# Twelve empty instructions ahead of VectorE's first fill, and the turn of b1's row five products later

## The chip, the cores and the metric

The kernel runs on one core of a Trainium2 chip. The metric is the device time of one execution in microseconds (us), as the median of the runs shown. Engine names in the profile: PE is TensorE's products and PEld its weight loads, DVE is VectorE, ACT is ScalarE, POOL is GpSimd, and SP is SyncE, which issues most transfers.

## The reference

A block with a local attention that is gated by a feed-forward layer: 2048 tokens, 448 columns, 16 heads of 28, all in bfloat16.

```python
x = A_x                                    # [1, 2048, 448]
xn = _layernorm(x, axis=-1)                # no scale, no shift
# attention: each token sees itself and 7 tokens before it, 2 apart
qkv = xn @ wqkv                            # [2048, 3 * 448]
idx = pos[:, None] - arange(8) * 2         # mask where idx < 0
attn = softmax(q . k[idx] * 28 ** -0.5)    # over the 8
s = (attn . v[idx]) @ wo
# feed-forward, F = 1792
h = gelu(xn @ w1 + b1)
g = silu(h @ w2 + b2)
return x + s * g
```

## The kernel before

The tokens are split into even and odd ones, so that a window with a step of 2 becomes a plain window in each half, and into 16 tiles of 128 tokens. Four tiles make a chunk of 512. Per tile, `norm` (L468) and `stats` (L428) take the row statistics on VectorE, scale x into a bfloat16 tile `xn`, and turn it on TensorE (tiles 0 to 3, against the identity `ident`) or by a transposing transfer (later tiles) into `xnT`, the layout that the products need. Since 448 columns are three blocks of 128 and one of 64, GpSimd copies the last 64 columns of `xn` a second time beside themselves (L480), and the second pair of transposes of each tile waits for that copy. `first_batch` (L605) makes the q, k and v products of tiles 0 and 1 block by block, as soon as half of a tile is turned. Products of the feed-forward layer, scores, weighted values and the output projection follow chunk by chunk; all of them are issued through `product` (L524).

The bias `b1` lies in memory as one row of 1792 numbers. A GpSimd transfer brings it as 14 rows of 128 (`b1r`, in the second buffer of the ring `E`, filled with zeros by GpSimd first: L418 and L419). TensorE turns these rows into a PSUM bank (`f_b1`, L1040 to L1042, task 223) and VectorE copies the 14 columns into `b1` (L1043, task 224). ScalarE reads `b1` first in the first gelu.

The order of the work is written out by hand. Every piece of work is a task of `_Plan`, with an engine, an estimated cost, what it depends on, and what buffers it takes and gives back. `ORDER` (L25) lists the task numbers, and each engine executes its own tasks in that order, so one task's place in the list decides what queues behind it on its engine. Semaphores are placed by the framework from what tasks read and write. `_place` also runs a clock of estimates: a task takes the buffer (a PSUM bank, say) that is estimated to be free earliest, and the warm-up products (tasks 1 to 48, with no use but to keep TensorE busy before x arrives) are left out when their estimated start is over 8.0. A transfer's estimated landing is its issue, its size over a rate, and a `tail`; tails are estimates alone and nothing in the program waits for them.

`zero` (L294) is the last buffer of the ring `h`; VectorE fills it with zeros as its first work (task 126, L1016), and seven rows of it go to memory as padding ahead of v once x's fourth tile has arrived. Behind that fill on VectorE stand the fills of `eps_t` and `half_t`, two of `qk_tok` and one of `v_tok`, and then the statistics of tile 0 (task 86). On TensorE, tasks around the turn are 134 (tile 0's second pair of transposes), 223 (b1's row), 159, 153 and 156 (tile 0's first products), 138 (tile 1's first transposes), 154 and 157 (two more products of tile 0) and 140 (tile 1's second transposes).

Of the kernel before, what the change touches and what calls it, by code (L numbers as in the profile page):

```python
# [11 lines left out]
ACT = mybir.ActivationFunctionType  # L12

HOP = 0.10
TABLE = 1.28
SWITCH = 0.095
AT_ONCE = ("DMA", "CLK")
INSIDE = {
# [5 lines left out]
BURST = 3.5  # L24
ORDER = [  # L25
# [74 lines left out]
class _Plan:  # L100
# [44 lines left out]
    def _place(self, t, way):  # L145
        assert not t.ndep
        e, c = t.eng[way], t.cost[way]
        last = self.free.get(e, 0.0)
        at = last + (SWITCH if e == "PE" and t.mode != self.mode else 0.0)
        got = {p: sorted(p.free)[:n] for p, n in t.take.items()}  # L150
# [4 lines left out]
        if load:  # L155
            at += TABLE
            self.table = t.table[0]
# [39 lines left out]
def kernel(  # L197
# [12 lines left out]
    nc = tc.nc  # L210
# [30 lines left out]
    def rows(halves, pos, n):  # L241
        h, r = divmod(pos, HALF)
        return halves[h, r:r + n, :]
# [50 lines left out]
    zero = p_h.bufs[27]  # L294
# [8 lines left out]
    plan = _Plan()  # L303
# [20 lines left out]
    def memset(eng, ap, v):  # L324
        def fn(_):
            getattr(nc, eng).memset(ap, v)  # L326
        return fn

    ones = nc.const_aps.tensor(1.0, (P, 512), BF16)
    t_on = plan.add("DMA", 0.7, lambda _: None)  # L330
# [28 lines left out]
    def dma(eng, dst, src, kb, deps=(), issue=0.45, rate=350.0, tail=1.7, share=0):  # L359
        def fn(_):  # L360
            i = {"SP": nc.sync, "ACT": nc.scalar, "POOL": nc.gpsimd}[eng].dma_start(dst, src)
            for d in deps:
                if id(d) in landing:
                    behind(i, landing[id(d)])
        ahead = [] if deps else in_turn
        a = plan.add(eng, issue, fn, [t_on] + list(deps) + [k for k, _ in ahead if k.eng == (eng,)][-1:], take=(p_q,) * share)
        d = plan.add("DMA", kb / rate, lambda _: None, [a], tail=tail, give=tuple((p_q, a, i) for i in range(share)))
        if kb > 50 and not deps:
            in_turn.append((a, d))
        return d  # L370
# [20 lines left out]
    def load_x(t0, n, eng="SP", deps=(), tail=1.6):  # L391
        src = rows(x_half, t0 * P, n * P).rearrange("(t p) d -> p t d", p=P)
        d = dma(eng, x_sb[:, t0:t0 + n, :], src, 112 * n, deps,
                rate=330.0 if t0 < 2 * TPC else 290.0, tail=tail, share=n if eng == "SP" else 0)
        for t in range(t0, t0 + n):
            t_x[t] = [d]
# [2 lines left out]
        return ap.rearrange("(k p) c -> p k c", p=P)  # L399


    load_x(0, 1, "SP", tail=1.1)
    load_x(1, 1, "ACT", tail=1.6)
    t_w = []

    def load_w(kt, tail, eng="SP"):
# [606 lines left out]
        for b in blocks_of[c]:  # L1013
            values(b)

    t_zero = plan.add("DVE", 0.27, memset("vector", zero[:], 0.0), [t_on])  # L1016
    t_vpad = dma("SP", v_hbm[:BACK, :], zero[:BACK, :], 7, [t_zero] + t_x[TPC - 1])
    project(0)

# [113 lines left out]
```

## Time and profile before

| what | us |
|---|---|
| median of 3 runs | 149.75 |
| lowest and highest | 149.12, 149.87 |
| the profiled execution, its own time | 148.96 |
| its span in the profile | 147.3 |
| TensorE products, busy | 142.1 (96% of the span) |
| VectorE, busy | 108.0 (73%) |
| ScalarE, busy | 102.2 (69%) |
| GpSimd, busy | 29.1 (20%) |

In rows of the timeline the first number is the start in us from the start of the span, the second the time from the first start to the last end of the row, then engine, line, operation, output and input, and how many instructions were merged (x3). In brackets stands how long the engine was idle before, and what ended that. Rows of the chain of waits have a start, a duration, and what the chain went through. In rows of transfers, the last number is the median time from issue to landing. "issue" is time in which an engine waited for nothing that the profile shows. Ends of products are modelled, and starts of consecutive products tell more than their durations.

### The profile page before, as it was taken

How to read it: one execution, taken by the hardware profiler on the slowest of the kernel's cores; microseconds unless marked ns; L12 is line 12 of the kernel's file. 1: busy time of each engine (PE TensorE's matmuls, PEld its weight loads, DVE VectorE, ACT ScalarE, POOL GpSimd, SP SyncE). 2: the span in 40 equal slices, each digit the busy share in tenths (PEclk: the TensorE clock that was granted, in tenths of full speed). 3: DMA queues.
4: the chain of work that ended last, by engine and by line, in shares of the span. 5: the costliest groups of instructions: out<-in, count | busy, mean ns of one | idle time of the engine just before them, and what ended most of it. 6: DMA issues, size and time to landing. Idle time of an engine off the chain costs nothing.

```text
span 147.3 us, 5467 instructions
## 1 busy us (share of the span) xinstructions
PE 142.1 (96%) x2266; PEld 88.4 (60%) x2266; DVE 108.0 (73%) x273; ACT 102.2 (69%) x190; POOL 29.1 (20%) x83
## 2 busy tenths in 40 slices
PE   7999999999999999999999999999999999999980
PEld 2457777788888875555555655446555454554550
DVE  2976720076965859499797987997989969689961
ACT  3447878876569556886988697799797497972330
POOL 4412511065550031102422010120001002000020
PEclk9999999999999999999999999999999999999999
DMA  4999966999998778899968638220011400000212
GB/s 103 379 320 317 119 142 141 289 184 302 261 162 163 105 152 73 190 134 179 161 129 176 160 89 187 91 71 4 6 52 30 134 20 4 0 23 28 78 62 65
DMA packets 39494, 19.47 MB, mean 132 GB/s; under 512 B 26631, under 2 KB 38762, under 8 KB 39470
## 3 DMA queue, kind: packets, MB, share of 16 engines
q1 hardware_dynamic: 38206, 17.25, 55.8%
q0 software_dynamic: 688, 1.31, 3.6%
q10 hardware_dynamic: 576, 0.57, 1.1%
q8 instruction: 17, 0.28, 0.9%
q14 instruction: 7, 0.06, 0.1%
HBM read 9.42 MB, written 3.94 MB: 91 GB/s over the span
## 4 chain that ended last, share of the span: by engine, by line
PE 92%; DVE 2%; DMA 2%; POOL 1%; issue 1%; DVEq 0%
PE bank L524 82%; PE bank L762 3%; PE bank L807 3%; PE bank L841 2%; DMA x_sb<-in_A_x_dram 2%; PE bank L940 1%; DVE st L430 1%; DVE sg L952 1%; DVE xn L473 0%; POOL head L354 0%; PE bank L507 0%; POOL xn L480 0%; POOL row L326 0%; DVE o L959 0%; DVE mv L434 0%
## 5 line engine op out<-in xcount | busy, mean ns | idle before, releaser
L524 PE MATMUL bank<-xnT,w 64*128 64x512 bf16 (+1 forms) x428 | 46.9, 376 | 0.0
L712 ACT ACTIVATE h<-bank,b 128x512 bf16<-128x512 f32 x56 | 35.6, 689 | 10.5 <-PE bank L524 10.0
L524 PE MATMUL bank<-w,h 64*128 64x448 bf16 (+1 forms) x440 | 41.8, 350 | 0.0
L524 PE MATMUL bank<-w_in,xnT 64*128 64x448 bf16 (+2 forms) x342 | 37.1, 350 | 0.0
L524 PEld LDWEIGHTS <-w 64*128 64x128 bf16 (+1 forms) x428 | 26.0, 93 | 14.4
L524 PEld LDWEIGHTS <-h 64*128 64x128 bf16 (+1 forms) x440 | 22.3, 93 | 11.7
L524 PEld LDWEIGHTS <-xnT 64*128 64x128 bf16 (+2 forms) x342 | 19.3, 94 | 11.1 <-issue 0.4
L816 ACT ACTIVATE E<-bank 128x456 bf16<-128x456 f32 (+1 forms) x36 | 17.6, 551 | 3.7 <-PE bank L807 3.6
L430 DVE BATCH_NORM_STATS2 st<-x_sb 128x6 f32<-128x448 bf16 x16 | 9.4, 607 | 13.2 <-DMA x_sb<-in_A_x_dram 13.2
L319 ACT CAST qk_tok<-bank 128x448 bf16<-128x448 f32 x26 | 13.0, 536 | 4.8 <-PE bank L524 4.8
L874 POOL COPY wide<-wide 64x64 bf16<-64x64 bf16 x20 | 5.8, 307 | 50.5 <-DVE wide L861 17.3
L853 DVE STREAM_TRANSPOSE wide<-bank 128x512 f32<-128x512 f32 x18 | 12.4, 703 | 3.0 <-PE bank L841 2.9
L878 DVE STREAM_TRANSPOSE oT<-wide 128x512 bf16<-128x512 bf16 x18 | 12.4, 696 | 0.6 <-POOL wide L874 0.2
L822 DVE TENSOR_TENSOR E<-E,m_gen 128x456 bf16<-128x456 bf16 (+1 forms) x32 | 11.9, 382 | 0.3 <-ACT E L816 0.3
L524 PE MATMUL bank<-wo,oT 64*128 64x448 bf16 x98 | 11.1, 349 | 0.0
L861 DVE TENSOR_TENSOR wide<-wide,rd 128x448 bf16<-128x448 f32 x18 | 10.7, 611 | 0.2
L774 DVE TENSOR_TENSOR wide<-bank,b 128x448 f32<-128x448 f32 x15 | 9.0, 610 | 1.8 <-PE bank L524 1.8
L692 ACT ACTIVATE kd<-qkT,head 128x1024 bf16<-128x1024 bf16 x8 | 9.1, 1147 | 1.0 <-DMA qkT<-qk_tok 1.0
L786 ACT ACTIVATE wide<-wide 128x448 f32<-128x448 f32 x12 | 6.8, 576 | 3.4 <-DVE wide L774 3.3
L841 PEld LDWEIGHTS <-v 64*32 64x32 bf16 x576 | 6.7, 89 | 3.6 <-issue 3.5
L319 ACT CAST v_tok<-bank 128x448 bf16<-128x448 f32 x12 | 6.4, 542 | 3.0 <-PE bank L524 2.2
L841 PE MATMUL bank<-E,v 64*32 64x57 bf16 (+1 forms) x576 | 7.6, 188 | 0.0
(80 smaller groups left out, 135.4 us busy)
## 6 DMA issues: line engine op xcount, KB each, us to landing
v<-v_hbm SPq DMA_DIRECT2D x17, 128.0 KB, 3.8
v_hbm<-v_tok SPq DMA_DIRECT2D x11, 128.0 KB, 3.3
w<-in_B_w_dram SPq DMA_DIRECT2D x2, 672.0 KB, 7.9
out_dram<-o SPq DMA_DIRECT2D x9, 112.0 KB, 1.8
x_sb<-in_A_x_dram SPq DMA_DIRECT2D x4, 224.0 KB, 4.8
w<-in_B_w_dram SPq DMA_DIRECT2D x2, 448.0 KB, 5.9
w_in<-in_A_wqkv_dram SPq DMA_DIRECT2D x2, 336.0 KB, 4.4
w<-in_B_w_dram SPq DMA_DIRECT2D x2, 336.0 KB, 6.4
```

The source lines that it names most:

```text
L319: nc.scalar.copy(o, i)
L430: nc.vector.bn_stats(out=buf(p_st, k)[:], in_=x_sb[:, t, :])
L524: return nc.tensor.matmul(ps[rows, :n], lhsT[:, rows], rhs, start=start, stop=stop)
L692: nc.scalar.activation(dst, src, ACT.Copy, scale=head[:, a:a + 1])
L712: nc.scalar.activation(buf(p_h, own, i)[:], buf(p_b, own, i)[:], ACT.Gelu_apprx_tanh, bias=b1[:, mt:mt + 1])
L774: nc.vector.tensor_tensor(out=buf(p_y, k)[:, :n], in0=buf(p_b, own, i)[:, :n], in1=b2[:, cs], op=ALU.add)
L816: nc.scalar.activation(buf(p_E, k)[:, :8 * n], buf(p_b, a, at + i)[:, :8 * n], ACT.Exp, scale=SCALE)
L822: nc.vector.tensor_tensor(out=E, in0=E, in1=m[:, :, :, :n].rearrange("p i g q -> p (i g) q"), op=ALU.mult)
L841: nc.tensor.matmul(banks[a][32 * g:32 * g + 32, c0:c0 + n], buf(*v_at[b])[r, s, 2 * g + h, :], buf(p_E, exps[2 * h + s // 2])[r, c1:c1 + n ...
L853: nc.vector.transpose(buf(p_dt, k)[:], buf(p_b, po, a)[:])
L861: nc.vector.tensor_tensor(out=turned_in(d[a]).rearrange("p l b c -> p (l b) c")[:, :, :DH], in0=buf(p_dt, d[a])[:].rearrange("p (b c) -> p ...
L878: nc.vector.transpose(oT[:, a::2, q:q + 256], turned_in(d[a]).rearrange("p l b c -> p l (b c)"))
```

## The change

Twelve `nop` instructions are issued on VectorE ahead of the fill of `zero`. In `ORDER`, task 223 moves from behind 134 to behind 157: past three products, tile 1's first transposes, and two more products. Task 224, its eviction, keeps its place. The estimated tails of the first two loads of x change.

```diff
+SPARE = 12
...
 ORDER = [
     64, 1, 82, 126, 49, 50, 83, 54, 52, 59, 66, 68, 72, 70, 2, 3, 4, 5, 6, 7, 74, 76, 78, 80, 102, 104, 106, 86, 87,
-    88, 90, 8, 9, 10, 11, 12, 13, 89, 129, 130, 51, 132, 85, 91, 92, 14, 15, 16, 17, 131, 134, 223, 55, 133, -136,
-    159, 153, 156, 93, 136, 138, -140, 108, 112, 114, 116, 154, 157, 94, 95, 96, 53, 97, 142, 224, 61, 62, 63, 137,
+    88, 90, 8, 9, 10, 11, 12, 13, 89, 129, 130, 51, 132, 85, 91, 92, 14, 15, 16, 17, 131, 134, 55, 133, -136, 159,
+    153, 156, 93, 136, 138, -140, 108, 112, 114, 116, 154, 157, 223, 94, 95, 96, 53, 97, 142, 224, 61, 62, 63, 137,
...
-    load_x(0, 1, "SP", tail=1.1)
-    load_x(1, 1, "ACT", tail=1.6)
+    load_x(0, 1, "SP", tail=1.4)
+    load_x(1, 1, "ACT", tail=1.3)
...
-    t_zero = plan.add("DVE", 0.27, memset("vector", zero[:], 0.0), [t_on])
+    def mk_zero(_):
+        for _ in range(SPARE):
+            nc.vector.nop()
+        nc.vector.memset(zero[:], 0.0)
+    t_zero = plan.add("DVE", 0.27, mk_zero, [t_on])
```

## The prediction

> **What bounds the kernel now.** I read the page's shares of the chain by engine, then the chain that ended last in order of time, then the first eight microseconds of the timeline and the busy time by stage.
>
> ```profile
> span 147.3 us, 5467 instructions
> PE 92%; DVE 2%; DMA 2%; POOL 1%; issue 1%; DVEq 0%
> ```
>
> TensorE (PE) carries 92% of the chain. The chain in order of time shows the rest, which lies at its two ends:
>
> ```profile
> 7.13 0.19 POOL xn L480
> ...
> 7.36 0.23 PE bank L507
> ...
> 141.01 1.37 PE bank L940 x8
> ...
> 143.13 0.20 DVE o L959
> 143.34 0.40 issue
> ```
>
> The reader sees a head (the chain runs from the load of x through VectorE's statistics, shown below, until GpSimd releases a transpose at 7.36) and a tail after TensorE, from 141.01 + 1.37 = 142.4. Between them TensorE does not rest. The busy time by stage (us of the stage, then PE, PEld, DVE, ACT, POOL) says so:
>
> ```profile
> 5.90:7.36 1.46, 1.32 (x10) 0.52 (x10) 1.30 (x5) 0.88 (x3) 1.12 (x7) 1.00 1.13 346
> 7.36:11.50 4.14, 4.14 (x40) 2.23 (x40) 2.93 (x11) 2.10 (x7) 0.48 (x2) 1.00 1.04 317
> 11.50:136.00 124.50, 124.50 (x2153) 79.13 (x2146) 94.03 (x228) 94.97 (x174) 24.41 (x61) 1.00 0.63 125
> ```
>
> So an edit in the head is worth exactly what it does to the 7.36, and an edit in the tail what it does after 142.4. Nothing that is hidden ahead of 7.36 counts.
>
> **The twelve empty instructions.** They stand ahead of the fill of `zero` (a buffer of h), VectorE's first work.
>
> ```profile
> 0.93 0.27 DVE L326 MEMSET h<- 128x256 uint32 x1 [0.93 <-PEq L1117]
> 1.15 0.06 DVE L326 MEMSET eps_t<- 128x1 f32 x1
> 1.33 0.11 DVE L326 MEMSET v_tok<- 128x64 bf16 x1
> 3.35 0.63 DVE L430 BATCH_NORM_STATS2 st<-x_sb 128x6 f32<-128x448 bf16 x1 [1.90 <-DMA x_sb<-in_A_x_dram]
> ```
>
> The trace has no empty VectorE instruction, so its price is bounded by the nearest rows: nothing, if it is dropped on the way to the chip, up to a first fill's 0.27 us. I take the smallest fill, 0.06, since no data is written: 12 x 0.06 = 0.72 us. Queued behind them are the six early fills, then the statistics. The fills end at 1.33 + 0.11 = 1.44 and would end at 2.16; the statistics wait for x until 3.35 in any case. The cover is the 1.90 us of idle time, and it is gone at 1.90 / 12 = 0.158 us each. The fills' other readers (ACT's square roots behind the statistics, the evictions of the first projections, the padding store behind x's fourth tile) come later still. Cost on the path: 0.
>
> **b1's row, five products later.** The row comes by a GpSimd DMA. Landing and turn:
>
> ```profile
> 1.37 0.72 POOL L361 DMA_DIRECT2D E<-in_B_b_dram  x1 [0.36 <-POOL E L326]
> E<-in_B_b_dram POOLq DMA_DIRECT2D x1, 3.5 KB, 4.4
> 5.53 0.29 DVE L321 COPY xnT<-bank 128x256 bf16<-128x256 bf16 x1
> 5.82 0.10 PEld L1041 LDWEIGHTS <-E 128*128 128x128 bf16 x1
> 5.83 0.23 PE L1041 MATMUL bank<-ident,E 128*128 128x128 bf16 x1
> 5.87 0.31 PEld L524 LDWEIGHTS <-xnT 128*128 128x128 bf16 x3
> ```
>
> The row lands at 1.37 + 4.4 = 5.77 and the turn begins at 5.82: here TensorE takes it the moment it is there. But the first product needs the copy that VectorE ends at 5.53 + 0.29 = 5.82, and loads at 5.87, the same 0.05 after its source. So taking the turn away frees its own start interval at most. That interval is 0.28 - 0.23 = 0.05 us by two transposes against one (0.28 is in the first row below). Then what follows is held by other work:
>
> ```profile
> 6.50 0.28 PE L507 MATMUL bank<-ident,xn 128*128 128x128 bf16 x2
> 6.04 0.40 DVE L473 TENSOR_SCALAR xn<-x_sb,mv,rstd 128x448 bf16<-128x448 bf16 x1
> 6.49 0.11 PEld L507 LDWEIGHTS <-xn 128*128 128x128 bf16 x2 [0.31 <-DVE xn L473]
> 6.62 0.54 PE L524 MATMUL bank<-w_in,xnT 128*128 128x448 bf16 x2
> 7.00 0.59 PE L507 MATMUL bank<-ident,xn 128*128 128x128 bf16 x2
> 7.08 0.23 POOL L480 COPY xn<-xn 128x64 bf16<-128x64 bf16 x1
> 7.36 0.10 PEld L507 LDWEIGHTS <-xn 128*128 128x128 bf16 x1 [0.45 <-POOL xn L480]
> 7.43 1.49 PE L524 MATMUL bank<-w_in,xnT 128*128 128x448 bf16 x7
> 8.07 0.17 DVE L1043 CAST b<-bank 128x14 f32<-128x14 bf16 x1
> ```
>
> Tile 1's first transposes wait for VectorE (6.04 + 0.40 = 6.44), and its last for GpSimd (7.08 + 0.23 = 7.31). The moved turn stands behind the two products of 6.62 and ahead of the transposes of 7.00: they go to 7.05, and the second still waits until 7.36, under the 0.45 us that the weight load sits idle there. The move passes no entry of SP's or GpSimd's queue; no DMA moves with it. Its eviction on VectorE stays at 8.07, behind tile 2's scaling; the bank is written by about 7.3, so it isn't late. What the move does buy is room for a late row. From the first product to the transpose of 7.36, TensorE has five products and three transposes. Seven products take 1.49 and two 0.54, so one more is (1.49 - 0.54) / 5 = 0.19 us. With transposes at 0.05 that is 1.10 in all, in 7.36 - 5.87 = 1.49: a row up to 0.39 later costs nothing before, each further 0.1 us costs 0.1; in the new place the room is about 7.2 - 5.77 = 1.4 us. In this execution: 0, at best 0.05.
>
> **Banks and tails.** The turn takes its PSUM bank later, so the names rotate by one. The bank it now takes was last used by a warm-up product, and the next users, tile 2's transposes behind the seven products of 7.43 (at 7.43 + 7 x 0.19 = 8.76), find banks whose copies have ended, b1's own at 8.07 + 0.17 = 8.24 among them. The two tails change the planner's landing of x0 by +0.3 and of x1 by -0.3 us; the order is written out, so they reach the program only through the choice of the bank that is free earliest and the warm-up limit of 8.0. By the planner's own arithmetic, with the costs in the code, task 163 (the product ahead of warm-up 18) ends at 8.03 before and about 8.16 after, so warm-up 18 and later are left out both times. 0 for both.
>
> **Where VectorE's instructions are fetched.** Twelve more instructions shift everything behind them in VectorE's stream. The page's instruction queues and the last instruction but one of VectorE:
>
> ```profile
> q8 instruction: 17, 0.28, 0.9%
> q14 instruction: 7, 0.06, 0.1%
> 143.13 0.39 DVE L959 TENSOR_TENSOR o<-x_sb,sg 128x448 bf16<-128x448 bf16 x1
> 143.73 0.26 DVE L952 TENSOR_TENSOR sg<-bank,w_in 128x96 bf16<-128x96 f32 x1 [0.21 <-issue]
> ```
>
> Programs come in blocks of about 0.06 MB / 7, some 8 KB. On the chain stand 0.40 us (0.21 of them VectorE idle) in which the last gating waited for nothing that the profile shows. If a block's edge makes that gap, the shift moves it ahead, where VectorE has time: a gain of 0.21 to 0.40. If it doesn't, 0; a gap that moves onto a bound place costs 0.40 at most. I take the 0.21, the nearer row, since no semaphore accounts for it. The Trainium skill (Runtime: NRT & Kernel Launch, Instruction fetch mechanics) says that a crossing of a block is one small step, mostly hidden; by that rule this term is 0 and the sum 149.75. Its blocks are 16 KiB; the trace has 16 KB on q8 and half that on q14.
>
> **Sum.** 0 + 0 + 0 - 0.21 on the profiled execution, 148.96 (147.3 of span and 1.66 around it), gives 148.75. The timed runs' median is 149.75, 0.79 above the profiled one; carried over, 149.75 - 0.21 = about 149.5.
>
> **Rivals.** (1) *The row is late in the timed runs.* TensorE takes the row 0.05 after landing, so it has no reserve, and some of the 0.79 us may be TensorE standing behind it: a landing 0.39 + 0.79 = 1.18 later would do. Then the move gives all of that back: 148.96. For it: nothing lies between landing and turn that could take up a delay but the 0.39. Against: the transfer took 4.4 us here, and nothing shows a longer one.
> (2) *The spread is TensorE's clock, and the move does nothing.* The warm-up products show a slow start:
>
> ```profile
> 2.08 0.15 PEld L334 LDWEIGHTS <-const-bfloat16-1.0 128*128 128x128 bf16 x1 [0.28 <-issue]
> 2.50 0.15 PEld L334 LDWEIGHTS <-const-bfloat16-1.0 128*128 128x128 bf16 x1 [0.28 <-issue]
> 5.33 0.39 PE L334 MATMUL bank<-const-bfloat16-1.0 128*128 128x128 bf16 x4
> ```
>
> 512 columns take 0.42 us at 2.08, half the rate of 0.19 for 448 later; 128 columns at 5.33 take (0.39 - 0.23) / 3 = 0.05, the full rate. The granted clock reads 1.00 throughout. If full rate comes after 7.36 in a timed run, the 1.10 us of work take 2.20 and end 2.20 - 1.49 = 0.71 late, nearly the whole excess; the turn costs the same in either place, and the time stays 149.75. The Trainium skill (TensorE: Matmul & The Clock Gate, The HAM clock gate) has the rise after about 3.4 us of work, in windows that do not start with the kernel; the trace agrees (half rate at 2.50, full rate by 5.33), and one trace cannot show the scatter.
> (3) *Slower: the empty instructions outlast the wait for x.* The point is 0.158 us each. At a first fill's 0.27 they take 3.24, 1.34 more than the cover, and the statistics, 7.36 and the end move by that: 151.1. Against: the smallest fill takes 0.06, and an empty instruction writes nothing.
> (4) *The empty instructions never reach the chip*, since nothing waits for them, or the gap in the tail is no block's edge: 149.75, with the move alone.
>
> **The numbers.** What a measurement of this kernel can tell from no change is about 0.5%, 0.75 us; the timed runs themselves spread from 149.12 to 149.87. Forecast 0.36, (1) 0.26, (2) 0.12, (3) 0.14, (4) 0.12. Faster: all of (1), and 0.07 of the forecast, where the whole 0.40 goes and the runs fall low: 0.33. Slower: (3), and 0.04 of the others, for a gap of 0.40 that moves onto a bound place in a slow draw: 0.18. Within: 0.49. The range goes from 148.96 - 0.40, about 148.6, to 149.87 + 0.40, about 150.3; it leaves out (3).
>
> **What would show it.** Right: statistics still at 3.35 and the last GpSimd-gated transpose at 7.36; the turn between 7.0 and 7.3, its weight load not waiting; the 0.40 of issue gone from the tail. Wrong: first statistics later than 3.4 (3), or a head that gets shorter than 7.36, or a bank wait on TensorE after it.

## The result, and the profile after

| | us, median | lowest to highest | runs |
|---|---|---|---|
| before, timed again beside the changed kernel | 149.34 | 148.92 to 152.84 | 21 |
| changed | 148.63 | 148.19 to 149.61 | 21 |

The ratio is 0.9957, with a 95% interval of 0.9941 to 0.9973: 0.71 us less between the medians, sure in sign, and under the 0.5% that the prediction calls no change. The time lies in the range given (148.6 to 150.3), near its lower end.

The profiled execution of the changed kernel happens to be its slowest run, 149.61, with a span of 147.6 against 147.3 before. So the two spans must not be subtracted; the profile has to be read stage by stage. First the head, in the chain of waits of the changed kernel (start, duration, what it went through) and the timeline of TensorE:

```profile
1.26 5.97 DMA w_in<-in_A_wqkv_dram
7.24 0.04 issue
7.28 0.73 PE bank L525 x3
```

```profile
7.28 0.73 PE L525 MATMUL bank<-w_in,xnT 128*128 128x448 bf16 x3 [1.10 <-DMA w_in<-in_A_wqkv_dram]
...
8.33 0.22 PE L1046 MATMUL bank<-ident,E 128*128 128x128 bf16 x1
8.39 0.28 PE L508 MATMUL bank<-ident,xn 128*128 128x128 bf16 x2
8.50 1.49 PE L525 MATMUL bank<-w_in,xnT 128*128 128x448 bf16 x7
```

In this execution a load of the projection weights landed late, at 7.24, and the first product waited 1.10 us for it. The seven products that began at 7.43 before begin at 8.50, 1.07 later. No edit touches that load, and no other profile of this study shows it waited for; so it is taken for an accident of this one execution. It lets one see how much the rest gained: 1.07 lost in the head, and a span only 0.3 longer.

The middle did not change. TensorE's last four products, in its timeline before and after:

```profile
142.84 0.33 PE L940 MATMUL bank<-wo,oT 128*128 128x96 bf16 x4
143.91 0.33 PE L941 MATMUL bank<-wo,oT 128*128 128x96 bf16 x4
```

From the seven products to the last four: 142.84 - 7.43 = 135.41 before, 143.91 - 8.50 = 135.41 after. What is left is the tail. The end of the chain of waits, before and then after:

```profile
143.34 0.40 issue
143.73 0.27 DVE sg L952
144.00 0.02 issue
144.03 0.21 DVE o L959
```

```profile
144.20 0.20 DVE o L960
144.40 0.08 issue
144.49 0.02 DVEq L960
144.51 0.00 issue
144.51 0.26 DVE sg L953
...
144.79 0.21 DVE o L960
```

The 0.40 us of issue ahead of VectorE's last gating is 0.08. From the start of the last four products to the end of VectorE's last instruction it took 144.03 + 0.21 - 142.84 = 1.40 us before and 144.79 + 0.21 - 143.91 = 1.09 after: 0.31 less. From there to the end of the span, while the last stores go out, it took 147.3 - 144.24 = 3.1 before and 147.6 - 145.00 = 2.6 after. The views of the transfers over the last 4 us show it, before and then after: the store on SyncE's queue takes less time from issue to landing (the last number).

```profile
out_dram<-o SPq DMA_DIRECT2D x1, 112.0 KB, 2.6
out_dram<-o SPq DMA_DIRECT2D x1, 112.0 KB, 1.9
```

Together the tail, from the start of the last four products to the end of the span, went from 147.3 - 142.84 = 4.5 to 147.6 - 143.91 = 3.7. That is the size of the whole difference between the medians. Two questions remain: what moved the gap, and whether TensorE's turn of b1's row had a part in it.

**What moved it was not the empty instructions.** The first line of each page, before and after, and the changed kernel's first VectorE instruction:

```profile
span 147.3 us, 5467 instructions
span 147.6 us, 5468 instructions
0.93 0.27 DVE L1020 MEMSET h<- 128x256 uint32 x1 [0.93 <-PEq L1122]
```

The changed kernel executes one instruction more, not twelve, and the first fill starts at 0.93 as before. The compiled programs have the same VectorE instructions but for one wait, and none of the twelve is in the changed one. Rows 23 and 27 of VectorE's program, before and after, with what each waits for:

```
23 L1043 CAST b_69<-bank_164 128x14 [waits PE_49]
27 L321 COPY xnT<-bank_161 128x2x128 [waits PE_49]

23 L1048 CAST b_69<-bank_161 128x14 [waits PE_49]
27 L322 COPY xnT<-bank_162 128x2x128 [waits PE_49,Activation_49]
```

As the turn stands later, the PSUM banks rotate by one, and the copy of tile 2's first half takes a bank whose semaphores make it wait for ScalarE as well as TensorE. The second wait becomes an instruction of its own on VectorE, and accounts for the one by which the page's count rises. The theory from here on (theory A): this one instruction shifts VectorE's stream against the blocks in which it is fetched, so that no block's edge stands at the last gating, and the turn's place in time is worth nothing. The rival (theory B): the turn's place on TensorE brings the gain.

### The profile page after: what moved, and what is told of

It reads as the page before. It is cut to its first block, busy times and chain, and to the rows that moved or that the text cites. A ratio compares the mean times of both kernels' runs of the same rounds, so it can differ in the third digit from the quotient of the medians.

```text
span 147.6 us, 5468 instructions
## 1 busy us (share of the span) xinstructions
PE 142.3 (96%) x2266; PEld 87.6 (59%) x2266; DVE 107.8 (73%) x273; ACT 101.9 (69%) x190; POOL 29.0 (20%) x83
## 4 chain that ended last, share of the span: by engine, by line
PE 92%; DMA 4%; DVE 1%; SPq 0%; issue 0%; DVEq 0%
PE bank L525 83%; DMA w_in<-in_A_wqkv_dram 4%; PE bank L763 3%; PE bank L808 3%; PE bank L842 2%; PE bank L941 1%; DVE sg L953 1%; PE bank L508 0%; DVE o L960 0%; SPq L362 0%; PE bank L761 0%; PE bank L492 0%; PE bank L1046 0%; DVEq L960 0%; DVEq L953 0%
## 5 line engine op out<-in xcount | busy, mean ns | idle before, releaser
L525 PEld LDWEIGHTS <-w 64*128 64x128 bf16 (+1 forms) x428 | 25.3, 93 | 15.1
```

The lines of the kernel that those rows point to most:

```text
L525: return nc.tensor.matmul(ps[rows, :n], lhsT[:, rows], rhs, start=start, stop=stop)
```

## Experiments

In the table the tail is counted as above, from the start of TensorE's last four products (its timeline) to the end of the span; "issue" is that of the chain ahead of the last gating; "fetch in the tail" says whether the page of the transfers over the last 4 us has a packet on q14, the instruction queue over which VectorE's program comes. Ratios are against runs of the kernel before on the same chip. The last column has the lowest of the timed runs.

| kernel | turn | median, ratio (interval) | tail | issue | fetch in the tail | lowest |
|---|---|---|---|---|---|---|
| before | old | 149.34, 1 | 147.3 - 142.84 = 4.5 | 0.40 | yes | 148.92 |
| changed | new | 148.63, 0.9957 (0.9941 to 0.9973) | 147.6 - 143.91 = 3.7 | 0.08 | yes | 148.19 |
| e1, old turn, one fill more | old | 148.51, 0.9962 (0.9941 to 0.9982) | 146.7 - 142.90 = 3.8 | 0.08 | yes | 148.31 |
| e2, new turn, one fill less | new | 149.22, 0.9992 (0.9969 to 1.0016) | 147.6 - 143.06 = 4.5 | 0.40 | yes | 148.79 |
| e3, old turn, twelve fills | old | 148.60, 0.9953 (0.9924 to 0.9982) | 146.4 - 142.83 = 3.6 | 0.09 | no | 148.04 |
| e4, new turn, twelve fills | new | 148.84, 0.9967 (0.9943 to 0.9991) | 146.4 - 142.88 = 3.5 | 0.08 | no | 148.13 |
| e5, 64 fills in the middle | old | one run | 153.2 - 149.64 = 3.6 | 0.09 | no | |
| e6, 128 fills in the middle | old | one run | 163.6 - 159.29 = 4.3 | 0.40 | yes | |
| e7, row late | old | one run | 149.5 - 145.23 = 4.3 | 0.40 | yes | |
| e8, row late | new | one run | 147.4 - 143.69 = 3.7 | 0.08 | yes | |
| e9, e4 and GpSimd's fills early | new | 148.69, 0.9944 (0.9915 to 0.9974) | 146.3 - 142.73 = 3.6 | 0.08 | no | 147.82 |
| e10, e3 and GpSimd's fills early | old | 148.34, 0.9947 (0.9917 to 0.9978) | 146.5 - 143.00 = 3.5 | 0.09 | no | 147.69 |

### One instruction more, one less (e1, e2)

e1 is the kernel before, with one more fill ahead of VectorE's first: the shift by one without the turn's move.

```diff
-    t_zero = plan.add("DVE", 0.27, memset("vector", zero[:], 0.0), [t_on])
+    def mk_zero(_):
+        nc.vector.memset(half_t[:], -0.5)
+        nc.vector.memset(zero[:], 0.0)
+    t_zero = plan.add("DVE", 0.27, mk_zero, [t_on])
```

> The kernel before with one more small fill (half_t a second time) ahead of VectorE's first; the turn stays where it was. Theory A (VectorE's stream: the changed kernel has one more instruction on VectorE, and that moves the edge of a block of instructions off the last gating and its fetch out of the last stores): as the changed kernel, 0.994 to 0.997 of before, the 0.40 of issue gone from the tail. Theory B (the turn's place on TensorE made the gain): 1.000, the 0.40 stays.

e2 is the changed kernel with one early fill handed to GpSimd: the turn's move without the shift.

```diff
-    t_eps = plan.add("DVE", 0.07, memset("vector", half_t[:], -0.5), [t_eps])
+    t_eps = plan.add("POOL", 0.07, memset("gpsimd", half_t[:], -0.5), [t_eps])
```

> The changed kernel with one small fill (half_t) moved from VectorE to GpSimd, so that VectorE's stream is as long again as before; the turn stays in its new place. Theory A: the gap of 0.2 to 0.4 ahead of the last gating comes back, and the time is 0.999 to 1.001 of before. Theory B: the gain stays, 0.996.

The tails in the chain of waits, e1 and then e2:

```profile
143.39 0.08 issue
143.47 0.02 DVEq L959
143.49 0.00 issue
143.50 0.26 DVE sg L952
```

```profile
143.35 0.20 DVE o L960
143.55 0.40 issue
143.95 0.27 DVE sg L953
```

One fill alone, with b1's row turned where it was, takes the 0.40 away and gives 0.9962; one instruction less, with the row turned in the new place, brings the 0.40 back, and the gain is gone (0.9992, the interval holds 1). With before and the changed kernel these are all four cases of turn and stream, and the gap and the time follow the stream. Theory B falls as the source of the gain; what the turn's place might add is too small for these intervals. And nothing is in the gap but the place in the stream: the instructions on either side of it are the same in all four.

### Twelve that do reach the chip (e3, e4)

Both kernels with twelve fills of the smallest kind where the change has its empty instructions (the edit of e1, in a loop of twelve).

> The kernel before with twelve more small fills ahead of VectorE's first, in the place of the twelve empty instructions, which do not show in the trace of the changed kernel. Theory A: the edge lies twelve instructions ahead of the tail; 0.992 to 0.996, the fetch lands before the last stores are issued; the statistics still start at 3.35, since twelve fills of 0.01 to 0.06 end by 2.2. Theory B: 1.000. The prediction's third rival (0.158 us each is the limit): slower only if the statistics start later than 3.35.

> The changed kernel with the twelve fills in front: both parts of the change, as its text reads. Theory A: as the old turn with twelve fills, 0.992 to 0.996, within 0.001 of it. Theory B: 0.996, as the changed kernel. If both add, 0.990.

VectorE's first rows in e3's timeline:

```profile
0.88 1.48 DVE L1018 MEMSET half_t<- 128x4 f32 x12 [0.88 <-PEq L1121]
2.36 0.27 DVE L1019 MEMSET h<- 128x256 uint32 x1
...
3.34 0.63 DVE L430 BATCH_NORM_STATS2 st<-x_sb 128x6 f32<-128x448 bf16 x1 [0.46 <-DMA x_sb<-in_A_x_dram]
```

The fills take 1.48 / 12 = 0.12 us each and are hidden: the statistics still start at 3.34, though only 0.46 of the 1.90 us of idle time is left. There is no packet on q14 in the last 4 us, and the tail is 3.6 and 3.5: another 0.1 to 0.2 below the changed kernel's. In the records of single packets, the last one on q14 begins at 139.02 in e3, at 144.54 in before and at 144.71 in after. These records also show that q14 is not VectorE's alone. Of its seven packets, those of before at 89.84 and 144.54 come at 80.80 and 139.02 in e3, where VectorE's stream is twelve longer; those at 44.59, 66.03 and 108.17 stay (44.02, 66.02, 108.12). Whose they are is not shown. The timed medians (0.9953, 0.9967) can't tell the two kernels from each other or from the changed one.

### How long a block is (e5, e6)

64 and 128 fills behind tile 8's statistics, in the kernel before. Theory A with blocks of 128 instructions (8 KB on q14) expects the edge to leave the gating by 64 and to come back to it by 128.

```diff
         def f1(k):
+            for _ in range(64 if t == 2 * TPC else 0):
+                nc.vector.memset(buf(p_st, k)[:], 0.0)
             nc.vector.bn_stats(out=buf(p_st, k)[:], in_=x_sb[:, t, :])
```

> The kernel before with 64 small fills on VectorE ahead of tile 8's statistics, where VectorE stands idle for 10.6 us waiting for x. Theory A with blocks of 128 instructions: the edge that stood at the last gating lies 64 instructions ahead of it; no gap there (0.08 of issue, not 0.40), the span as the changed kernel's kind, 146.2 to 146.9.

> The same with 128 fills. Theory A with blocks of 128: the next edge stands exactly where the old one stood, so the 0.40 of issue is back ahead of the last gating and the fetch is in the last stores again; span 147.0 to 147.6. A rival, that any more instructions ahead help (a fixed lead of the sequencer): no gap, as with 64.

The tail in the chains, e5 and then e6, and the fills in e5's timeline with the product that waited behind them:

```profile
150.14 0.09 issue
150.22 0.02 DVEq L961
150.24 0.26 DVE sg L954
```

```profile
159.79 0.40 issue
160.19 0.27 DVE sg L954
```

```profile
29.80 8.35 DVE L431 MEMSET st<- 128x6 f32 x64
...
39.92 1.83 PE L526 MATMUL bank<-xnT,w 64*128 64x512 bf16 x8 [4.87 <-DVE v_tok L321]
```

The gap goes with 64 and returns with 128, 0.40 as before: the period is one that fits into 128 and not into 64, which is 128 itself. The 128 fills also bring one packet on q14 more, eight for seven; with 8 KB for a block that makes 64 bytes for an instruction. The expected whole times were missed (154.9 and 165.59, beside 149.49 for before on that chip): the fills came behind the statistics' wait for x, not under it, took 0.13 each and held an eviction for which TensorE waited. The granted clock of the two executions reads 0.987 and 0.948, against 1.00. The tail's reading does not depend on that.

What inside a crossing takes the 0.40 is open. The gating does not wait for the packet seen in the tail: that packet begins 0.79 to 0.81 us behind the gating's start in before, e2, e6 and e7 (144.54 for 143.73 in before). By this order it brings a later part of the program.

### A late row (e7, e8)

Eight more fills of the row's buffer on GpSimd ahead of its transfer, in the kernel before and in the changed one: this tests the room for a late row that the prediction counted, 0.39 us in the old place and 1.4 in the new.

```diff
-    t_b1z = plan.add("POOL", 0.1, memset("gpsimd", b1r, 0.0), [t_on])
+    def mk_b1z(_):
+        for _ in range(9):
+            nc.gpsimd.memset(b1r, 0.0)
+    t_b1z = plan.add("POOL", 0.1, mk_b1z, [t_on])
```

> The kernel before with eight more fills of b1's row tile on GpSimd ahead of the row's transfer, so that it is issued about 1.6 us later and lands at 7.2 to 7.5. By the prediction's count the old place has 0.39 us of room: the first product starts behind the landing, and the last transpose of tile 1 moves from 7.36 to about 8.4; span 148.2 to 148.5, with the 0.40 in the tail as before.

> The changed kernel with the same late row. The new place has about 1.4 us of room: products start at 5.9 as with an early row, and the last transpose of tile 1 comes at 7.4 to 7.6; span 146.6 to 146.9. If the turn's place had no worth even with a late row, it would move as far as the old one, to about 8.4.

TensorE's timeline, e7 and then e8:

```profile
8.21 0.23 PE L1044 MATMUL bank<-ident,E 128*128 128x128 bf16 x1 [1.89 <-DMA E<-in_B_b_dram]
8.27 0.73 PE L527 MATMUL bank<-w_in,xnT 128*128 128x448 bf16 x3
...
9.44 0.73 PE L527 MATMUL bank<-w_in,xnT 128*128 128x448 bf16 x3
```

```profile
5.86 0.74 PE L528 MATMUL bank<-w_in,xnT 128*128 128x448 bf16 x3
...
8.10 0.23 PE L1049 MATMUL bank<-ident,E 128*128 128x128 bf16 x1 [0.96 <-DMA E<-in_B_b_dram]
8.17 0.28 PE L511 MATMUL bank<-ident,xn 128*128 128x128 bf16 x2
8.28 1.49 PE L528 MATMUL bank<-w_in,xnT 128*128 128x448 bf16 x7
```

In the old place a row that is there at 8.20, 2.43 late, puts the products behind tile 1 from 7.43 to 9.44, 2.01 later; the prediction's count gives 2.43 - 0.39 = 2.04. In the new place a row at 8.10, 2.33 late, puts them from 7.43 to 8.28, 0.85 later; the count gives 2.33 - 1.4 = 0.93. So the move does buy about a microsecond of room: with the late row, the products behind tile 1 start 2.01 - 0.85 = 1.16 us sooner for it. Between the two single runs, 151.31 and 149.23, lie 2.08, but 4.3 - 3.7 = 0.6 of that is the tail. Both rows were later, and both spans longer, than expected: the nine fills took 2.30 us, 0.26 each. No profile without those fills shows TensorE waiting for the row, and e1 and e2 leave nothing in the timed runs for it.

### A shorter head on top (e9, e10)

With the tail settled, the head was tried: GpSimd's fills for `head` and `row` move from 5.55 to 7.0, where they held tile 1's copy (L480), into its idle time ahead of 5.45.

```diff
-    88, 90, 8, 9, 10, 11, 12, 13, 89, 129, 130, 51, 132, 85, ...
+    88, 90, 8, 9, 10, 11, 12, 13, 89, 129, 130, 51, 61, 62, 63, 132, 85, ...
```

> The changed kernel with twelve more fills on VectorE (as e4) and with GpSimd's fills for the head and the row taken right behind its first loads' fills, into idle time of GpSimd ahead of 5.45. Theory C (the end is the block edge and the stores; all else is the dense stretch that starts when tile 1's last copy is done): the products behind tile 1 start some 0.3 us sooner, at 7.05 to 7.10 instead of 7.36, the tail from TensorE's last product stays at 3.4, and the time is 0.3 us under e4's: 148.4 to 148.5, 0.993 of before. Rival: the products wait for x's loads or the weights instead, and the start stays at 7.3 to 7.4: as e4, 0.995 to 0.997.

> The same with the turn in its old place (as e3, with GpSimd's fills early). Theory C: products behind tile 1 0.3 us sooner, tail 3.4, 0.992 to 0.994 of before. Rival: the start is held by the loads, and the time is that of e3, 0.995. The turn's place itself is expected to be worth under 0.1 us between this run and e9.

GpSimd's copy and TensorE's timeline in e9; the last line is the one of e4 that answers to the second:

```profile
6.50 0.24 POOL L481 COPY xn<-xn 128x64 bf16<-128x64 bf16 x1 [0.81 <-DVE xn L474]
5.40 0.63 PE L335 MATMUL bank<-const-bfloat16-1.0 128*128 128x128 bf16 x4
...
6.02 0.73 PE L525 MATMUL bank<-w_in,xnT 128*128 128x448 bf16 x3
...
7.25 1.49 PE L525 MATMUL bank<-w_in,xnT 128*128 128x448 bf16 x7
```

```profile
5.26 0.39 PE L335 MATMUL bank<-const-bfloat16-1.0 128*128 128x128 bf16 x4
```

The copy runs at 6.50 instead of about 7.0 and no longer holds anything: from the first product to the seven it takes 7.25 - 6.02 = 1.23 us, near the 1.10 that the prediction counts as TensorE's own work there, against 7.36 - 5.80 = 1.56 in e4. But the first product came 0.22 later in this execution than in e4: the warm-up products ahead of it ran 0.63 instead of 0.39 for four. So the start of the seven moved by 0.11 (7.25 for 7.36) and not by the 0.3 expected; in e10 it moved by 0.18 (7.23 for 7.41 in e3). The lowest timed runs are 0.3 below those of e3 and e4 (147.69 and 147.82 against 148.04 and 148.13), the medians are not; the intervals of all kernels whose tail lost the edge overlap. Whether the early fills are worth something is left open, and none of these versions is shown to beat the changed kernel.

## Why the prediction came out as it did

**The gap in the tail as a block's edge: right.** It was argued only from 0.40 us of issue without a releaser and 7 packets of 8 KB, of which most are not VectorE's. e1 and e2 make and unmake it with one instruction, e6 brings it back after 128. By the Trainium skill's rule (Runtime: NRT & Kernel Launch, Instruction fetch mechanics) a crossing is mostly hidden, and that gave 149.75: it fails here at the tail, where the engine is the bound and 0.31 us stand on the path. Ahead of the tail a crossing costs no time, since TensorE is the bound there, but it can be seen. In before the block ahead of the last one begins with the instruction behind a gating of 0.62 us, which hides the crossing; in the changed kernel, one instruction sooner, it begins with that gating itself, which starts from idle. The gating, before and then after:

```profile
88.69 0.62 DVE L954 SCALAR_TENSOR_TENSOR sg<-bank,g 128x448 bf16<-128x448 f32 x1 [0.19 <-PE bank L524]
90.11 0.62 DVE L955 SCALAR_TENSOR_TENSOR sg<-bank,g 128x448 bf16<-128x448 f32 x1 [0.55 <-ACT kd L693]
```

VectorE stands idle 0.36 longer ahead of it, and about as much in e1 and e8 (0.57 and 0.55). (The releaser named after is not the cause: before, the same work of ScalarE ended at 88.78, behind the gating's start.)

**What shifts the stream: wrong.** The step "twelve more instructions shift everything behind them" failed; the empty instructions never reach the chip, which was the first half of rival (4). What failed with it is "banks and tails: 0". It looked at whether a bank would be free in time, and that was right; but another bank meant another set of waits, and one wait more is one instruction more. The sign came out right because any shift of the stream by a few instructions moves the edge off the gating: one, twelve and sixty-four all did. That was luck in the carrier; rival (4), which gave 149.75 in that case, missed the same wait.

**The size: too small.** The term was taken at 0.21, VectorE's idle time, within 0.21 to 0.40. Measured, VectorE's end came 0.31 sooner, and the stores behind it some 0.5 sooner, which was not in the sum at all. In the records of single packets, the last of the 16 shares of before's last store landed at 146.32, 0.60 behind the fifteenth (145.72), while a fetch packet of 0.60 us lay beside the stores from 144.54; after, the last share was 0.18 behind the fifteenth. The store on SyncE's queue shows how. In before, e2, e6 and e7 the fetch begins 0.12 to 0.15 behind its first packet; 120 of its 128 packets of data then end early, and the other eight, one share of sixteen, end from 0.03 or 0.04 us behind the fetch's end on (145.17 for 145.14 in before). The store takes 1.06 to 1.30 us from first packet to last there and 0.48 to 0.61 in the other eight kernels, where the fetch has ended ahead of it or is not in the tail. So the share stands behind the fetch on its transfer engine. No run moved the packet without moving the edge. In e3, e4, e5, e9 and e10, without a fetch there, the tail is the shortest (3.5 to 3.6); why those of the changed kernel, e1 and e8 are 0.1 to 0.3 longer, with the fetch over before that store begins, is open.

**The sum.** 149.5 stands 0.87 above 148.63. Of that 0.41 is the base: 149.75 was the median of three runs, and 21 runs have 149.34. The other 0.46 is the term: 0.71 between the medians against 0.25 taken.

**The empty instructions at 0, the turn at 0: right numbers.** That twelve instructions fit under the wait for x holds even for real fills (e3), at 0.12 each and not the 0.06 taken. Those fills write one buffer, and each waits by a semaphore for the one ahead of it; the first fills of before, into different buffers, start only 0.01 to 0.07 apart behind the first (1.15, 1.16, 1.19, 1.26, 1.33). For fills that wait for each other, rival (3)'s point, 0.158, is near. The turn's place alone is worth nothing that these runs can tell (e2), and its room came out as counted (e7, e8). The steps to be seen were: the statistics at 3.35, seen at 3.34; the 0.40 gone, seen; the transpose at 7.36, not seen in the disturbed profile, but e4 has the new turn, at 6.92, just ahead of the 7.0 to 7.3 given, and the seven products at 7.36 behind it (7.43 before).

**The other rivals.** (1), the row late in the timed runs, falls with e1: the whole gain without the move. (2), the clock, is not the cause of this change's gain, but a part of it is real: the warm-up products ahead of the first transposes take 0.39 in some profiles and 0.63 in others, which moves the head by about 0.2. How much of the spread of the timed runs that is stays open, as does how often a weight load is late as in the profile of after.

## What to carry to other kernels

When an edit of no cost changes the time by a fraction of a microsecond, look at the last instructions of the engine that ends the kernel for "issue" without a releaser, and add or take away one instruction early in its stream: if the gap goes, the edge of a block of instructions made it. Count a change's instructions in the profile before costing them; one that does nothing may not be there, and one that only moves can bring a wait with it, since another buffer has other waits. And read an edge near the end twice, for the engine that stalls and for the stores that a fetch can hold up.

## What the runs showed of the hardware

- VectorE's stream comes in blocks of 128 instructions, 8 KB (e1, e5, e6); where an edge stood at its last gating (before, e2, e6, e7), 0.40 us of issue lay ahead of it, and 0.08 or 0.09 in all others.
- An instruction fetch of 0.50 to 0.66 us beside the last stores held up one share of sixteen of a 112 KB store, which took 1.06 to 1.30 us for 0.48 to 0.61.
- An empty instruction without a semaphore is not in the compiled program and took neither time nor a place in the stream: 5468 instructions against 5467, the one being a wait.
- Fills of 128 x 4 or 128 x 6 into one buffer, busy 0.06 us each and each waiting for the one before, took 0.12 to 0.13 each (e3, e5).
- One transfer of weights landed at 7.24 in one profile (5.97 on the chain, with 1.10 us of TensorE waiting), and TensorE had taken up its work without that wait in the others; four 128-column warm-up products took 0.39 us at about 5.3 in before, e1 to e4 and e8, and 0.61 to 0.63 in after, e5 to e7, e9 and e10. The mean granted clock does not tell the two apart: it reads 1.00 in after and e7 as in before.
